# Attention with hashed buckets, then a mixture of experts: a group's first product with v issued one step earlier, and one more block transposed by DMA

## The chip, the cores and the metric

The kernel runs on one core of a Trainium2 chip. The metric is the device time of one execution in microseconds. The kernel before was timed three times: 747.42, 748.88 and 756.24 us, median 748.88 us. One further execution was profiled; its page and its trace are what this document reads.

Engines are named as in the profile: PE is the tensor engine (PEld its loading of weights), DVE is VectorE, ACT is ScalarE, POOL is GpSimd, and SP is the queue of SyncE, which issues most DMAs. L265 is line 265 of the kernel before.

## The reference

Attention with 4 batches, 8 heads, 768 positions and 64 channels per head. A query sees only the keys that fall into the same bucket, and the bucket is the sign pattern of six projections. The 512 channels of each of the 3072 tokens then go to one of 8 experts, the one with the largest gate logit.

```python
q_bits = (np.einsum('bhsd,dk->bhsk', q, proj) > 0)          # the same for k
mask = q_bucket[:, :, :, None] == k_bucket[:, :, None, :]
scores = np.where(mask, scale * np.matmul(q, k.transpose(0, 1, 3, 2)), -1e9)
attn = np.exp(scores - scores.max(-1)); attn = attn / (attn.sum(-1) + 1e-9)
x = np.matmul(attn, v)                       # [4, 8, 768, 64] -> [3072, 512]
expert_idx = np.argmax(x @ w_gate, axis=1)   # one expert of 8 for each token
out = gate_w * (np.maximum(x @ w1[e], 0) @ w2[e])            # e: the token's expert
```

## The kernel before

**Groups, blocks, steps.** Attention runs over 16 pairs of heads (`pr`, four pairs for each batch), and each pair over two halves of the queries (`g`). A pair and a half, written (pr, g), is a group; there are 32. A group has six blocks, (jj, hh): three tiles of 128 queries times the pair's two heads. A block is 128 queries by all 768 keys. The main loop (L752) takes one block a step, 192 steps in all; `n`, from 0 to 5, is the step inside its group.

**What a step issues.** Step i issues, in this order:

- turns that are due: DVE transposes a block that came back from a DMA (L256, into `pt`);
- what `later` holds for this step (DMAs of a moved block, the scaling of the sign bits on ACT);
- loads of v (step 0 of a second half) and of q and k for the pair after the next;
- the scores of block i + 2, called S here: four matmuls on PE (L225, L226) into one of two banks `s`, then the row maximum and two small operations on DVE (L228 to L230);
- the exponential of block i + 1 on ACT (L240), with its row sums;
- what `late` holds: ACT copies the finished product `o` to `ot` (L290) and adds 1e-9 to the row sums (L291);
- six PE transposes of block i, called T here (L265), three into each of two banks `t`, each three followed by a copy on ACT into `pt` (L268);
- at some steps a product with v (L283, `av`): 24 matmuls that add one query tile of the group before into the bank `o`;
- pieces of the routing (`timed`), then `out_and_route` when it is due, then what PREPARE lists for the next pair.

PE, DVE, ACT and SP take their instructions in exactly this order (a manual schedule); on POOL the work on q, k and the scattered rows is chained in the same order (`in_turn`).

**Blocks moved by DMA.** MOVES lists groups in which one or two blocks aren't transposed by PE. Their exponential is written as `pd`, four DMAs on SP write it to DRAM (L250, when the exponential's step begins), one DMA reads it back in another order two steps later (L253), and DVE finishes the transpose three steps after that (L256). In groups 2 to 7 the block of step 1 is moved, in groups 8 to 28 those of steps 1 and 3. `blocks` gives each group the order of its blocks and the order of its three products: (0, 1, 2) without moves, (1, 0, 2) with one move, (1, 2, 0) with two.

**Products.** The three products of a group stand in steps 1, 3 and 5 of the next group. In step 5, after the third, `av_evac` arranges the evacuation: for all groups but the last three it goes to `late`, so that ACT does it in step 0; for (14, 1) and (15, 0) DVE does it at once (L293, L301, L302). The list `divide` keeps the reciprocal of the row sums, and `out_and_route`, four steps after the evacuation was arranged, does whatever that list holds. There is one bank `o`.

**Routing.** After the last pair of a batch, `out_and_route` starts the gate logits of the half (L334, PE and a copy on ACT), and pieces follow at 1, 2, 3, 4, 5 and 7 steps: the output rows (L315, L316), gathering, the best expert (L358, L359), its one-hot (L363 to L367), ranks among the tokens (L373 to L384), and three scattered DMAs on POOL (L392). These fall into the first two pairs of the next batch. For the second half of the last batch the logits of three of the four pairs are made early (`early_logits`, L493 to L508), once (14, 1) is evacuated.

**Preparing the next pair.** PREPARE gives, for each step of a pair, which operands of the next pair are made: `q_operands` and `k_operands` on POOL, the projections and sign bits `pair_codes` (PE L148 into a bank `t`, DVE L150 into `cr`; ACT scales `cr` two steps later, L151), and `code_rows`, four DMAs on SP for each head (L176). For most pairs the codes are made in step 1 of the first half and the two heads' rows go out in step 4 and in step 0 of the second half.

**The rest.** Behind attention come the experts, two matrix products each in three passes, with weights loaded on SP and split on ACT and DVE (the first weights are split on DVE and POOL beside pairs 14 and 15: L679, L682).

Of the kernel before, what the change touches and what calls it, by code (L numbers as in the profile page):

```python
# [8 lines left out]
F32 = mybir.dt.float32  # L9
# [9 lines left out]
P = 128  # L19
B, H, S, D = 4, 8, 768, 64  # L20
NB = S // P
NPAIR = H // 2
# [35 lines left out]
def lsh_attention_moe_kernel(ctx, tc, qkd, q2d, k2d, v, pjbd, wg, w1, w2, ident_in, tri_in, cols_in, eoff_in, ids_in, out):  # L58
# [216 lines left out]
    late = []  # L275
    divide = []

# [8 lines left out]
    def av_evac(pr, g, sums, o, defer):  # L286
# [11 lines left out]
        if defer:  # L298
            divide.append(lambda: V.reciprocal(out=inv, in_=sums.rearrange("p (j h) -> p j h", h=2)))
        else:  # L300
            V.tensor_scalar(out=sums, in0=sums, scalar1=1e-9, scalar2=None, op0=ALU.add)  # L301
            V.reciprocal(out=inv, in_=sums.rearrange("p (j h) -> p j h", h=2))  # L302
# [210 lines left out]
    MOVES = {}  # L513
    for n in range(2, 2 * NPR - 3):
        MOVES[divmod(n, 2)] = (1, 3) if n >= 2 * NPAIR else (1,)
# [27 lines left out]
    for hh in range(2):  # L543
# [6 lines left out]
        {(0, 0): [(q_operands, (0,))], (0, 1): [(pair_codes, ()), (q_operands, (1,))], (0, 2): [(k_operands, (0,))], (0, 3): [(code_rows, (0,)), (k_operands, (1,))],  # L550
         (0, 4): [(code_rows, (1,))]})
    grp = {}
# [173 lines left out]
    def out_and_route(pr, g):  # L726
        while divide:
            divide.pop(0)()
        if pr % NPAIR < NPAIR - 1:
# [22 lines left out]
    for i, (pr, g, jj, hh) in enumerate(steps):  # L752
# [47 lines left out]
        for x in now:  # L800
            timed.remove(x)
            if x[1].__name__ == "gather_heads":
                x[1]()
        if prev is not None:
            if n == 0:
                o = ps_o.tile([P, 512], F32, name="o")
            order_p = blocks(prev[0], prev[1])[1]
            for jp in (order_p[:2], order_p[2:])[n] if last and n < 2 else order_p[n // 2:n // 2 + 1] if not last and n % 2 == 1 else ():
                av(prev[0], prev[1], jp, o)
            if n == (1 if last else 5):  # L810
                av_evac(prev[0], prev[1], prev[2], o, (prev[0], prev[1]) != (NPR - 2, 1) and not last)
                if not last:
                    due.append((i + 4, lambda a=prev[0], c=prev[1]: out_and_route(a, c)))
                if (prev[0], prev[1]) == (NPR - 2, 1):
                    light += early_logits(B - 1, 1)
        if n == 5:
            prev = (pr, g, sums)

        for x in now:
# [31 lines left out]
        if due and due[0][0] == i:  # L851
            due.pop(0)[1]()
        for f, x in PREPARE[2 if pr == NPR - 2 else min(pr, 1)].get((g, n), ()) if pr + 1 < NPR else ():
            f(pr + 1, *x)
# [376 lines left out]
```

## Time and profile before

| what | value |
|---|---|
| median of three runs | 748.88 us |
| profiled execution | 746.31 us |
| its span, first to last instruction | 744.5 us |
| mean granted clock of PE over the span | 0.993 |
| PE busy | 717.5 us, 96% |
| DVE, ACT, POOL busy | 527.4, 457.9, 384.5 us |
| idle time of PE | 27 us: 744.5 less 717.5 |

Attention takes the first 460 us, with the routing between the batches; the experts take the rest. A row of a timeline gives the start in us, the busy time in us, the engine, the line, the operation, the tile written and the tiles read, the shape, the number of merged instructions, and in brackets the idle time of that engine just before and what ended it. Starts of PE's instructions are records, their ends are modelled, so distances are best taken from start to start. Some PE records also overlap: a matmul starts while the one before it drains.

### The profile page before, as it was taken

The page shows a single profiled execution, that of the slowest core. Times are in us where ns is not written, and L with a number is a line of the kernel's source. Part 1 is how long each engine was busy: PE and PEld are TensorE (multiplying, and loading weights), DVE is VectorE, ACT ScalarE, POOL GpSimd, SP SyncE. Part 2 cuts the span into 40 slices and gives each one's busy share as a digit, 9 for nine tenths or more (in the row PEclk, how much of TensorE's full clock was granted, in tenths as well). Part 3 has the DMA queues.
Part 4 walks back from the last instruction along what each step waited for, and adds up shares of the span by engine and source line. Part 5 has one row for each costly group of instructions (what it writes and reads, how often), then busy time and mean ns, then how long its engine had stood idle before and what let it go on. Part 6 is the DMA issues. An engine that isn't in the chain of part 4 may idle for free.

```text
span 744.5 us, 16345 instructions
## 1 busy us (share of the span) xinstructions
PE 717.5 (96%) x5919; PEld 632.3 (85%) x5919; DVE 527.4 (71%) x1158; ACT 457.9 (62%) x941; POOL 384.5 (52%) x366
## 2 busy tenths in 40 slices
PE   6999999999999999999989998999999999999996
PEld 3788888877888778888777887999999999999994
DVE  6667776887887888887899776674747465566741
ACT  5888887777888678888677865343434334344430
POOL 2877337098436187634485242007474738364381
PEclk8999999999999999999999999999999999999999
DMA  5166666666666567666664531746556565657531
GB/s 185 50 192 165 195 182 189 187 194 189 178 183 190 170 203 196 166 181 188 176 180 131 160 90 59 209 105 177 146 175 152 189 165 161 188 154 226 165 91 43
DMA packets 85259, 121.45 MB, mean 163 GB/s; under 512 B 10758, under 2 KB 57382, under 8 KB 85168
## 3 DMA queue, kind: packets, MB, share of 16 engines
q1 hardware_dynamic: 80176, 107.61, 51.3%
q0 software_dynamic: 4992, 12.69, 4.9%
q8 instruction: 49, 0.80, 0.5%
q14 instruction: 42, 0.34, 0.1%
HBM read 79.04 MB, written 39.24 MB: 159 GB/s over the span
## 4 chain that ended last, share of the span: by engine, by line
PE 45%; issue 22%; POOL 13%; DVE 11%; DMA 5%; SPq 2%; ACT 1%; POOLq 0%; DVEq 0%
PE o L283 14%; POOL y L1007 10%; PE t L265 9%; PE s L225 9%; PE s L226 7%; DVE m L228 4%; DMA y<-yo,tags 2%; POOL yo L1005 1%; PE misc L315 1%; PE t L148 1%; DMA qk<-qkd 1%; DMA xr<-xs 1%; DVE m L230 1%; SPq L176 1%; ACT p L240 1%
## 5 line engine op out<-in xcount | busy, mean ns | idle before, releaser
L228 DVE TENSOR_REDUCE m<-s 128x1 f32<-128x768 f32 x192 | 182.6, 951 | 48.4 <-PE s L226 41.4
L240 ACT ACTIVATE p<-s,m 128x768 f32<-128x768 f32 x144 | 143.3, 995 | 42.0 <-DVE m L230 27.8
L225 PE MATMUL s<-k,q 128*128 128x512 f32 (+1 forms) x384 | 149.2, 389 | 7.8 <-ACT p L240 5.2
L283 PE MATMUL o<-pt,vt 128*64 128x128 f32 x2304 | 146.7, 277 | 0.2
L268 ACT COPY pt<-t 128x384 f32<-128x384 f32 x288 | 123.9, 482 | 34.3 <-PE t L265 31.2
L283 PEld LDWEIGHTS o<-pt,vt 128*64 128x64 f32 x2304 | 123.8, 137 | 14.8 <-issue 7.4
L226 PE MATMUL s<-k,q 76*128 76x512 f32 (+1 forms) x384 | 123.9, 343 | 0.2 <-DVE q L218 0.2
L265 PE MATMUL t<-ident,p 128*128 128x128 f32 x864 | 120.0, 274 | 3.2 <-DVE cr L150 3.1
L1007 POOL DMA_INDIRECT y<-yo,tags x89 | 103.3, 1161 | 25.2 <-issue 22.9
L225 PEld LDWEIGHTS s<-k,q 128*128 128x128 f32 x384 | 73.2, 191 | 44.4 <-issue 15.0
L265 PEld LDWEIGHTS t<-ident,p 128*128 128x128 f32 x864 | 99.0, 141 | 6.7 <-DVE cr L150 4.0
L965 ACT ACTIVATE hh<-hps 128x352 fp32r<-128x352 f32 (+3 forms) x56 | 28.0, 500 | 99.3 <-PE hps L979 88.6
L682 DVE TENSOR_TENSOR wlo<-wraw,whi 128x1024 fp32r<-128x1024 f32 x60 | 73.0, 1219 | 17.0 <-ACT whi L677 16.0
L226 PEld LDWEIGHTS s<-k,q 76*128 76x128 f32 x384 | 73.7, 192 | 9.3 <-ACT k L201 0.5
L998 PE MATMUL hps<-hh,wlo 128*128 128x436 f32 (+6 forms) x224 | 76.2, 340 | 0.0
L998 PE MATMUL hps<-hh,whi 128*128 128x448 f32 (+10 forms) x224 | 76.2, 340 | 0.0
L998 PE MATMUL hps<-hl,whi 128*128 128x436 f32 (+6 forms) x224 | 76.2, 340 | 0.0
L979 PE MATMUL hps<-xh,whi 128*128 128x352 f32 (+3 forms) x224 | 75.0, 335 | 0.0
L979 PE MATMUL hps<-xh,wlo 128*128 128x428 f32 (+6 forms) x224 | 74.8, 334 | 0.0
L979 PE MATMUL hps<-xl,whi 128*128 128x428 f32 (+6 forms) x224 | 74.8, 334 | 0.0
L1005 POOL TENSOR_TENSOR yo<-yt,tags 128x512 f32<-128x512 f32 (+3 forms) x25 | 23.4, 959 | 88.1 <-DVE yt L1000 88.0
L966 DVE SCALAR_TENSOR_TENSOR hl<-hps,hh 128x352 fp32r<-128x352 f32 (+3 forms) x56 | 31.7, 566 | 48.6 <-ACT hh L965 45.0
(225 smaller groups left out, 1202.1 us busy)
## 6 DMA issues: line engine op xcount, KB each, us to landing
wraw<-w SPq DMA_DIRECT2D x64, 512.0 KB
moved<-pd SPq DMA_DIRECT2D x192, 96.0 KB
pq<-moved SPq DMA_DIRECT2D x48, 384.0 KB
qk<-qkd SPq DMA_DIRECT2D x30, 384.0 KB
xs<-zrow SPq DMA_DIRECT2D x8, 910.0 KB
vt<-v SPq DMA_DIRECT2D x16, 384.0 KB
xr<-xs SPq DMA_DIRECT2D x12, 178.8 KB
xr<-xs SPq DMA_DIRECT2D x8, 227.5 KB
```

Source lines behind the costliest of these rows:

```text
L225: PE.matmul(out=s[:, c0:c1], lhsT=q1[:, qs], rhs=k1[:, c0:c1], start=True, stop=False)
L226: PE.matmul(out=s[:, c0:c1], lhsT=q2[0:KM, qs], rhs=k2[0:KM, c0:c1], start=False, stop=True)
L228: V.reduce_max(out=m[:, 0:1], in_=s[:, 0:S], axis=AX.X)
L240: A.activation(to, of, AF.Exp, bias=m[:, 2:3], scale=m[:, 1:2], accum_out=sums[:, idx:idx + 1])
L265: PE.transpose(out=t[:, i * P:i * P + P], in_=p[:, kc * P:kc * P + P], identity=ident)
L268: A.copy(out=dst, in_=src)
L283: PE.matmul(out=o[hh * D:hh * D + D, jj * P:jj * P + P], lhsT=vt[:, kc, hh * D:hh * D + D], rhs=pt[:, hh, kc], start=kc == 0, stop=kc == N ...
L682: loeng.tensor_tensor(out=lo[:, i:i + step], in0=cell["t"], in1=bf(hi[:, i:i + step]), op=ALU.subtract)
L966: V.scalar_tensor_tensor(out=hl, in0=hps[:, 0:C], scalar=0.0, in1=bf(hh), op0=ALU.max, op1=ALU.subtract)
L979: PE.matmul(out=hps[:, 0:w], lhsT=wt[:, c, fs], rhs=xt[:, c, 0:w], start=n == 0, stop=n == 3 * NDC - 1)
L998: PE.matmul(out=yps[:, 0:w], lhsT=wt[:, f, ds], rhs=ht[:, 0:w], start=n == 0, stop=n == 3 * NFC - 1)
L1007: rows_apart("out", G.indirect_dma_start(out=out_seg, out_offset=bass.IndirectOffsetOnAxis(ap=tags[:, i, 0:1].bitcast(I32), axis=0), in_=y ...
```

## The change

The first of a group's three products is issued in step 5 of the group itself, behind the T of that step; `o` is allocated there. The other two stand in steps 1 and 3 of the next group. The evacuation is arranged in step 3, so that ACT does it in step 4. `out_and_route` comes six steps after that instead of four, which is the same step as before; since two groups' reciprocals can now be pending, `divide` is keyed by group. For the last group the two products left of the group before stand in its steps 0 and 1, where three stood.

Group (0, 1) joins MOVES, with the block of its step 1. Its blocks and its products then follow the order of the groups with one move. There are 49 moved blocks instead of 48.

For pairs 5, 9 and 13 PREPARE makes the codes of the next pair in step 3 of the first half instead of step 1, and the first head's code rows go out in step 5 instead of step 4.

```diff
-    divide = []
+    divide = {}
...
-            divide.append(lambda: V.reciprocal(out=inv, in_=sums.rearrange("p (j h) -> p j h", h=2)))
+            divide[(pr, g)] = lambda: V.reciprocal(out=inv, in_=sums.rearrange("p (j h) -> p j h", h=2))
...
-    for n in range(2, 2 * NPR - 3):
+    for n in range(1, 2 * NPR - 3):
         MOVES[divmod(n, 2)] = (1, 3) if n >= 2 * NPAIR else (1,)
...
-         (0, 4): [(code_rows, (1,))]})
+         (0, 4): [(code_rows, (1,))]},
+        {(0, 0): [(q_operands, (0,))], (0, 1): [(q_operands, (1,))], (0, 2): [(k_operands, (0,))], (0, 3): [(pair_codes, ()), (k_operands, (1,))],
+         (0, 5): [(code_rows, (0,))], (1, 0): [(code_rows, (1,))]})
...
-        while divide:
-            divide.pop(0)()
+        if (pr, g) in divide:
+            divide.pop((pr, g))()
...
-        if prev is not None:
-            if n == 0:
-                o = ps_o.tile([P, 512], F32, name="o")
-            order_p = blocks(prev[0], prev[1])[1]
-            for jp in (order_p[:2], order_p[2:])[n] if last and n < 2 else order_p[n // 2:n // 2 + 1] if not last and n % 2 == 1 else ():
-                av(prev[0], prev[1], jp, o)
-            if n == (1 if last else 5):
+        at = (0, 1) if last else (1, 3)
+        if prev is not None and n in at:
+            av(prev[0], prev[1], blocks(prev[0], prev[1])[1][1 + at.index(n)], o)
+            if n == at[1]:
                 av_evac(prev[0], prev[1], prev[2], o, (prev[0], prev[1]) != (NPR - 2, 1) and not last)
                 if not last:
-                    due.append((i + 4, lambda a=prev[0], c=prev[1]: out_and_route(a, c)))
+                    due.append((i + 6, lambda a=prev[0], c=prev[1]: out_and_route(a, c)))
...
         if n == 5:
             prev = (pr, g, sums)
+            if not last:
+                o = ps_o.tile([P, 512], F32, name="o")
+                av(pr, g, blocks(pr, g)[1][0], o)
...
-        for f, x in PREPARE[2 if pr == NPR - 2 else min(pr, 1)].get((g, n), ()) if pr + 1 < NPR else ():
+        for f, x in PREPARE[2 if pr == NPR - 2 else 3 if pr > NPAIR and pr % NPAIR == 1 else min(pr, 1)].get((g, n), ()) if pr + 1 < NPR else ():
```

## The prediction

> **What bounds the kernel now.** I read the page first, then busy time by stage, then the timelines of single steps. The page's engine line and its TensorE slices:
>
> ```profile
> PE 717.5 (96%) x5919; PEld 632.3 (85%) x5919; DVE 527.4 (71%) x1158; ACT 457.9 (62%) x941; POOL 384.5 (52%) x366
> ...
> PE   6999999999999999999989998999999999999996
> ```
>
> TensorE (PE) is busy 717.5 of 744.5 us. The change removes almost no work from it, so it can win only where PE stands idle, and there is little of that: the first slice, the last, and the 8s in the middle. Busy time of stretches that I cut at the score products shows where the 8s lie (columns: length, then PE, PEld, DVE, ACT, POOL busy with counts, clock, DMA share, GB/s): an ordinary pair (pair 6), then pairs 4 and 5, which follow a batch's end and carry its routing.
>
> ```profile
> 178.54:203.77 25.23, 25.23 (x256) 21.51 (x254) 20.54 (x45) 20.78 (x46) 14.07 (x14) 1.00 0.61 173
> ...
> 120.81:178.54 57.73, 54.42 (x544) 44.59 (x542) 47.00 (x126) 42.51 (x95) 33.00 (x31) 1.00 0.66 194
> ```
>
> Pair 6 has no PE idle time at all. Two pairs with routing take 57.73 instead of 2 x 25.23 = 50.46 us and hold 3.31 us of idle time. In the ordinary stage an operation that is only moved costs or wins nothing unless it makes PE wait.
>
> **The first groups.** The change puts the first product with v of group (0,0) into its own step 5, behind that step's transposes, and lets the block of step 1 of group (0,1) be moved by DMA. PE's timeline there (S = L225 with L226, T = L265, product = L283):
>
> ```profile
> 26.34 0.82 PE L265 MATMUL t<-ident,p 128*128 128x128 f32 x6
> 27.89 0.50 PE L225 MATMUL s<-k,q 128*128 128x512 f32 x1 [0.73 <-ACT p L240]
> ...
> 28.71 0.82 PE L265 MATMUL t<-ident,p 128*128 128x128 f32 x6
> 29.62 0.50 PE L225 MATMUL s<-k,q 128*128 128x512 f32 x1
> ...
> 30.43 0.82 PE L265 MATMUL t<-ident,p 128*128 128x128 f32 x6
> 31.18 1.53 PE L283 MATMUL o<-pt,vt 128*64 128x128 f32 x24
> 32.64 0.50 PE L225 MATMUL s<-k,q 128*128 128x512 f32 x1
> ```
>
> ```profile
> 30.47 0.99 ACT L240 ACTIVATE p<-s,m 128x768 f32<-128x768 f32 x1
> ```
>
> ScalarE paces this stretch, and PE waits. Start to start, S to T is 0.82 (27.89 to 28.71), T to product 0.75 (30.43 to 31.18), product to S 1.46 (31.18 to 32.64). T to S, where nothing waits, is 0.55 (in pair 10, below, T to T is 1.37, less 0.82). After the change: T at 26.34, product at 27.09, S at 28.55, T at 29.37, S at 29.92, no T, product 0.82 later at 30.74, next S at 32.2. Today that S starts at 32.64 with one product done; then it would start 0.44 earlier with two done. It also needs the exponential of the block whose S is at 27.89, which starts 2.58 behind that S (30.47): with S at 28.55 it runs from 31.13 to 32.12, and its sum is read a little later, so I put that S at 32.4. The gain is 1.46 + 0.24 = 1.7 us. It stays, because PE's slices from there to the first 8s are full and every group still holds three products; it is cashed where the last group has one product less in front of it. Bounds: 1.46 + 0.44 = 1.9 if that exponential comes sooner; a loss of 0.7 if the whole delay of S (28.55 for 27.89) falls on the chain and the early product is worth nothing. I take 1.7, since every step of it is in these rows.
>
> The move itself adds one turn on VectorE, four writes and one read on SP's queue.
>
> ```profile
> L256 DVE STREAM_TRANSPOSE pt<-pq x48: 967/969/979, 54.3 to 413.7; 128x768 f32<-128x768 f32 x48
> ...
>   DMA pq<-moved: 2.2, 3
> ```
>
> ```profile
> 32.39 0.71 SPq L176 DMA_DIRECT2D k<-cr  x1
> ...
> 42.46 1.78 SPq L250 DMA_DIRECT2D moved<-pd  x4
> ```
>
> The turn is 0.97 us in group (1,0), where it replaces ScalarE's two copies; of 48 turns 3 waited for their read, 2.2 us together. The four writes (1.78 in the row above, those of step 1 of (1,0)) will stand on SP ahead of the second head's code rows, whose last now goes out by 33.10, of the loads of pair 2 and a prefill; all of these become some 2 us later. The second head's first S is in step 0 of (1,0), a step ahead of the writes at 42.46, so near 40: 5 us of cover remain. If it were gone, PE would lose what is missing, once: 0 to 2 us, taken as 0.
>
> **The ordinary groups.** Products stay in steps 1, 3 and 5, so PE's load by step is the same. Two things get tighter. First, ot and the sums are evacuated in step 4 instead of step 0, ahead of that step's copies, and step 5 turns again at once. PE and then ScalarE in pair 10:
>
> ```profile
> 295.65 0.82 PE L265 MATMUL t<-ident,p 128*128 128x128 f32 x6
> ...
> 297.02 0.82 PE L265 MATMUL t<-ident,p 128*128 128x128 f32 x6
> ```
>
> ```profile
> 295.02 0.99 ACT L240 ACTIVATE p<-s,m 128x768 f32<-128x768 f32 x1 [0.24 <-DVE inv L299]
> ...
> 296.18 0.86 ACT L268 COPY pt<-t 128x384 f32<-128x384 f32 x2
> ...
> 299.05 1.01 ACT L240 ACTIVATE pd<-s,m 128x768 f32<-128x768 f32 x1
> ...
> 300.03 0.49 ACT L290 COPY ot<-o 128x384 f32<-128x384 f32 x1
> 300.39 0.24 ACT L291 ACTIVATE sums<-sums 128x6 f32<-128x6 f32 x1
> 300.58 0.86 ACT L268 COPY pt<-t 128x384 f32<-128x384 f32 x2
> ```
>
> Behind an exponential, ot starts after 0.98 (299.05 to 300.03) and the copies 0.55 later. In step 4 that would put the copies at 295.02 + 1.53 = 296.55 instead of 296.18: 0.37 late. The pair of copies ends at 297.04 now; its first half frees a bank near 296.7, and T of step 5 starts at 297.02 with its second half some 0.3 later: 0.3 of slack for 0.37 of delay. All but the last three of the 32 groups are evacuated this way. Between 0 and the 0.07 that these numbers leave I take 0.02 us, 0.5 over 29 groups, since a copy that waits for its T loses less than one that ScalarE paces. Bounds: 0 if the slack holds, 29 x 0.37 = 10.7 us if it is gone.
>
> Second, the product of the moved block stands in step 3 instead of 5, one step behind its turn. In group (6,1):
>
> ```profile
> 195.38 0.97 DVE L256 STREAM_TRANSPOSE pt<-pq 128x768 f32<-128x768 f32 x1
> ...
> 197.65 1.53 PE L283 MATMUL o<-pt,vt 128*64 128x128 f32 x24
> ```
>
> The turn ends at 196.35, and the product that stands there now begins at 197.65: 1.3 us of cover. Behind that product on PE's queue stands the S of step 4, and the exponential behind that waits with it. In (5,0), below, the cover is 0.6. Only a read landing over 0.6 late would show, and then VectorE itself waits with it, as today. Price 0, up to 2.2 us (today's waits once more).
>
> **The pairs with routing.** In pairs 5, 9 and 13 the sign bits (pair_codes) go from step 1 to step 3, the first code rows from step 4 to 5. Group (5,0), VectorE and then PE:
>
> ```profile
> 155.88 0.62 DVE L150 TENSOR_SCALAR cr<-t,cols 128x384 fp32r<-128x384 f32 x1
> 156.41 0.97 DVE L256 STREAM_TRANSPOSE pt<-pq 128x768 f32<-128x768 f32 x1
> ...
> 161.12 0.56 DVE L316 TENSOR_TENSOR xr<-misc,inv 128x384 f32<-128x384 f32 x1
> 161.59 0.95 DVE L228 TENSOR_REDUCE m<-s 128x1 f32<-128x768 f32 x1
> ```
>
> ```profile
> 153.35 0.85 PE L148 MATMUL t<-qk,pj 128*32 128x384 f32 x8
> ...
> 156.55 0.55 PE L265 MATMUL t<-ident,p 128*128 128x128 f32 x3 [0.94 <-DVE cr L150]
> ...
> 157.97 1.53 PE L283 MATMUL o<-pt,vt 128*64 128x128 f32 x24
> 159.75 0.52 PE L315 MATMUL misc<-ident,ot 128*128 128x128 f32 x3 [0.24 <-DVE slot L384]
> 160.02 0.48 PE L225 MATMUL s<-k,q 128*128 128x512 f32 x1
> ...
> 162.17 0.50 PE L225 MATMUL s<-k,q 128*128 128x512 f32 x1 [0.53 <-ACT p L240]
> ```
>
> T waits 0.94 us for a bank that cr still holds. Without cr in step 1, VectorE is 0.53 ahead (155.88 to 156.41) until step 3. But the projection (0.85 of PE, 153.35) is moved too, behind L315, which waits for VectorE. L315 then starts at 159.75 - 0.53 = 159.22, the projection 0.27 later, S at 160.34 instead of 160.02 and its T at 161.16; xr starts at 160.59, cr behind it near 161.1 and is done at 161.7. T's second bank waits for that instead of 161.45, and the S of 162.17 starts at about 162.0. Late next is cr again, two steps on. I take 0 for each of the three pairs; bounds 0.5 worse (cr's 0.53 now stands ahead of step 4's maximum) to 0.94 + 0.53 = 1.47 better (both waits gone). On SP the code rows wait for ScalarE's scaling in step 5, with the load of v and the second head's rows behind them; their first use is five steps on.
>
> **The end.** The product with v of (14,1) ends two steps earlier, so the early logits leave step 5 of (15,0), where PE waits for ot.
>
> ```profile
> 437.24 0.83 PE L493 MATMUL misc<-ot,wg_sb 128*32 128x384 f32 x2 [0.43 <-DVE ot L293]
> ...
> 439.57 2.84 PE L283 MATMUL o<-pt,vt 128*64 128x128 f32 x48
> ```
>
> ```profile
> 436.64 0.55 DVE L293 COPY ot<-o 128x384 f32<-128x384 f32 x1
> 437.10 0.79 DVE L301 TENSOR_SCALAR sums<-sums 128x6 f32<-128x6 f32 x1
> ```
>
> Of the two products at 439.57 one is already done, which is the gain counted above; the 0.43 us of waiting go as well. Against it, ot, L301 and the reciprocal come into step 3 of (15,0), beside the casts of w1. L301 took 0.79 for 6 columns. [...] From the rows alone: gain 0.43, less 0 to 0.8. I take 0.4.
>
> **Sum.** 1.7 + 0.4 - 0.5 = 1.6 us less. The profiled execution took 746.31 (span 744.5 and 1.8 around it), which gives 744.7. The median of the runs, 748.88, is 2.57 above the profiled one, so 747.3.
>
> **Rivals.** (1) Slower: the evacuation in step 4 makes T of step 5 wait. It decides from the point where the copies come over 0.3 us later than now. For it: 0.37 against 0.3. Against: a copy that waits for T loses less, and 0.3 covers most of the 0.37. Half its bound, 29 x 0.18 = 5.3, gives 747.3 + 4.8 = 752.1, the whole 757.5. (2) Faster: in pairs 5, 9 and 13 the wait really goes, 3 x 1.47 = 4.4: 742.9. For it: VectorE is the late engine there. Against: PE's moved projection. (3) The early start is worth nothing: the S that slips by 0.66 carries through ScalarE, and only the 0.43 and the 0.5 remain: 749.0. For it: ScalarE paces those steps. Against: one turning and its copies are gone there.
>
> **How the numbers follow.** Forecast 0.5, rival (1) 0.18, (2) 0.17, (3) 0.15. The range 742.0 to 752.0 holds the forecast, (2), (3) and the half of (1) in which less than half the slack is missing: about 0.9, less some 0.1 for the runs' own spread (747.42 to 756.24). About 2%, 15 us, is what a measurement of this kernel can tell from no change; even rival (1) in full stays inside it. Faster by over 2%: 0.02; within: 0.95; slower: 0.03, for a stall of every group that no row shows.
>
> **What would show it.** Right: no idle of 0.73 near 27.9; L256 x49 and L265 x858; one product, not two, ahead of the second S of the last group; no wait of L493 for ot. Rival (1): L265 waiting for L268 in step 5. Rival (2): pairs 4 and 5 clearly under 57.73. Rival (3): two products ahead of the S that now starts at 32.64, and that S over a microsecond later. The prediction is wrong if ordinary pairs leave 25.23, or if L283 waits for L256.

## The result and the profile after

The changed kernel is slower. Its median is 760.01 us (751.69 to 761.63, seven executions) against 750.41 us (747.42 to 758.11, seven) for the kernel before in the same series: a ratio of 1.0119, 95% interval 1.0079 to 1.0158. The prediction was 747.3 us, range 742.0 to 752.0. These numbers can't be understood without the clock: six of the seven executions of the changed kernel show a mean clock of TensorE (PE) of 0.980 to 0.983 and 759.51 to 761.63 us, while the profiled one has 0.992 and 751.69 us, so its trace shows only part of the loss, 5.38 us over the 746.31 profiled before.

The page of the changed kernel, engines and PE's slices:

```profile
PE 720.6 (96%) x5913; PEld 632.9 (84%) x5913; DVE 526.8 (70%) x1159; ACT 455.0 (61%) x939; POOL 387.9 (52%) x366
...
PE   6999999999999899999899998999999999999996
...
PEclk9999999999999999999989999999999999999999
```

PE is busy 3.1 us longer, with six transposes (one T) fewer, and its clock has a dent in the middle that the page of before does not have (that one has an 8 in its first slice). Busy time by stretches cut at S (length, then PE, PEld, DVE, ACT, POOL busy, clock, DMA share, GB/s) shows where. The kernel before, pairs 4 and 5, 8 and 9, 12 and 13, then pairs 6 and 7, then group (15,1):

```profile
116.44:174.17 57.73, 54.43 (x545) 44.59 (x544) 46.91 (x125) 42.11 (x94) 32.91 (x31) 1.00 0.69 203
224.67:281.77 57.10, 54.39 (x545) 44.60 (x544) 47.51 (x126) 42.38 (x94) 33.42 (x32) 1.00 0.64 187
332.27:390.32 58.05, 54.46 (x546) 44.58 (x544) 48.77 (x126) 42.45 (x95) 33.73 (x33) 1.00 0.63 183
174.17:224.67 50.50, 50.50 (x508) 43.02 (x509) 42.39 (x92) 41.67 (x91) 27.82 (x25) 1.00 0.62 178
431.61:451.15 19.54, 19.11 (x202) 15.12 (x201) 13.80 (x34) 10.94 (x24) 6.73 (x6) 1.00 0.24 74
```

The changed kernel, the same five:

```profile
115.12:172.72 57.60, 54.87 (x545) 44.67 (x544) 46.76 (x125) 41.48 (x94) 32.82 (x31) 1.00 0.65 197
223.69:281.83 58.14, 54.72 (x546) 44.63 (x544) 48.66 (x126) 41.94 (x95) 33.70 (x33) 1.00 0.61 182
332.68:393.80 61.12, 57.33 (x545) 46.50 (x544) 47.55 (x126) 42.05 (x95) 33.66 (x33) 0.94 0.59 174
172.72:223.69 50.97, 50.97 (x509) 42.97 (x509) 42.40 (x92) 41.44 (x91) 27.76 (x25) 1.00 0.62 179
435.45:454.02 18.57, 17.27 (x178) 13.78 (x177) 13.17 (x34) 10.94 (x24) 6.77 (x6) 1.00 0.25 79
```

The changed kernel comes into pair 4 1.32 us ahead, wins 0.97 in the last group, and loses 4.0 in the three routed stretches (-0.13, +1.04, +3.07) and 0.47 in four ordinary groups. The last S ends 2.87 us later than before (454.02 for 451.15), and 2.5 us more are lost behind it: PE waits 0.80 us there for the late rows of the first expert (0.08 before), the rest was not traced. The 3.07 holds a halved clock, which follows a window in which PE waited 1.56 us for a bank. Halved for 6.82 us while PE works all through, it costs up to half of that, 3.4 us, by estimate:

```profile
369.60:373.02 3.42, 1.86 (x17) 1.45 (x14) 3.14 (x14) 2.00 (x4) 3.28 (x4) 1.00 0.72 225
373.02:379.84 6.82, 6.80 (x45) 4.44 (x44) 4.67 (x14) 3.71 (x11) 6.43 (x7) 0.50 0.78 228
```

### The profile page after: what moved, and what is told of

Its sections match the earlier page's. It is cut to its first block, busy times and chain, and to the rows that moved or that the text cites. A ratio compares the mean times of both kernels' runs of the same rounds, so it can differ in the third digit from the quotient of the medians.

```text
span 749.9 us, 16376 instructions
## 1 busy us (share of the span) xinstructions
PE 720.6 (96%) x5913; PEld 632.9 (84%) x5913; DVE 526.8 (70%) x1159; ACT 455.0 (61%) x939; POOL 387.9 (52%) x366
## 5 line engine op out<-in xcount | busy, mean ns | idle before, releaser
L228 DVE TENSOR_REDUCE m<-s 128x1 f32<-128x768 f32 x192 | 182.6, 951 | 52.0 <-PE s L226 39.7
L283 PE MATMUL o<-pt,vt 128*64 128x128 f32 x2304 | 148.3, 278 | 0.0
L1009 POOL DMA_INDIRECT y<-yo,tags x89 | 105.7, 1188 | 25.2 <-issue 22.6
L265 PEld LDWEIGHTS t<-ident,p 128*128 128x128 f32 x858 | 97.1, 141 | 4.9 <-issue 1.9
```

The lines of the kernel that those rows point to most:

```text
L228: V.reduce_max(out=m[:, 0:1], in_=s[:, 0:S], axis=AX.X)
L265: PE.transpose(out=t[:, i * P:i * P + P], in_=p[:, kc * P:kc * P + P], identity=ident)
L283: PE.matmul(out=o[hh * D:hh * D + D, jj * P:jj * P + P], lhsT=vt[:, kc, hh * D:hh * D + D], rhs=pt[:, hh, kc], start=kc == 0, stop=kc == N ...
L1009: rows_apart("out", G.indirect_dma_start(out=out_seg, out_offset=bass.IndirectOffsetOnAxis(ap=tags[:, i, 0:1].bitcast(I32), axis=0), in_=y ...
```

## The experiments

They ran in five series, each on one chip with the kernel before beside it; its medians were 739.07, 752.77, 737.85, 737.72 and 737.53 us. "Low" below counts the executions with a mean clock under 0.99.

### First series: the parts alone

The first theory came from the dent above: idle time of PE in the routed pairs brings the clock down. Four kernels hold parts of the change: all but the codes' place, the codes' place alone, the shifted products alone, the moved block alone.

```diff
# e1_codes_back, against the kernel after
-        for f, x in PREPARE[2 if pr == NPR - 2 else 3 if pr > NPAIR and pr % NPAIR == 1 else min(pr, 1)].get((g, n), ()) if pr + 1 < NPR else ():
+        for f, x in PREPARE[2 if pr == NPR - 2 else min(pr, 1)].get((g, n), ()) if pr + 1 < NPR else ():
# e2_codes_only: the kernel before with that line of the kernel after, and its fourth table
# e3_products_only: e1 with     for n in range(2, 2 * NPR - 3)
# e4_move_only: the kernel before with     for n in range(1, 2 * NPR - 3)
```

> The changed kernel with the sign bits of pairs 5, 9 and 13 back in step 1 and their first code rows back in step 4; products, evacuation and the move of (0,1) as changed. Theory A (clock): the moved sign bits leave the tensor engine idle for 1.56 us in one stretch of pair 13's group (13,0), and its clock is then halved for 6.83 us there, and in most runs in pairs 5 and 9 as well; with the bits back no halved clock between 30 and 740 us, granted clock 0.99, and 746 to 751 us. Theory B (ScalarE): the evacuation in step 4 and the shifted products cost the time; then this stays at 757 to 761. Theory C (the moved block of (0,1)): also 757 to 761.

> The kernel before with only the sign bits of pairs 5, 9 and 13 moved to step 3 (first code rows to step 5). Theory A: granted clock 0.98 in most runs, halved stretches of 6.83 us near pairs 5, 9 and 13, 756 to 761 us. Theories B and C: as before, 747 to 751, clock 0.99.

> The kernel before with only the first product in step 5, the others in steps 1 and 3, and the evacuation in step 4. Theory A: 747 to 752, clock 0.99; against before about 1 us more in the groups with two moved blocks and 1 us less at the start. Theory B: 757 to 761. Theory C: as before.

> The kernel before with only the block of step 1 of group (0,1) moved by DMA. Theories A and B: 0.5 to 1 us less than before in the first two pairs, 746 to 751 us, clock 0.99. Theory C: 757 or more.

Measured: 738.31 us (ratio 0.9997, 0.9913 to 1.0081), 738.85 (0.9995, 0.9921 to 1.0068), 743.12 (1.0011, 0.9914 to 1.0108), 737.19 (0.9983, 0.9898 to 1.0069). Low: 1 of 4, 0 of 4, 2 of 4, 1 of 4, and 2 of 7 for the kernel before. None is told apart from it, and the kernel before has low executions too: the low clock is not new with the change.

### Second series: the changed kernel again, and idle time filled

```diff
# f1_changed_again: the kernel after.  f2_codes_back_again: e1.
# f3_changed_filled and f4_before_filled: the kernel after and before, with
+        if pr > NPAIR and pr % NPAIR == 1 and n in (1,):
+            fill(pr, o, 4)      # 4 x PE.matmul(out=o[:, 384:512], lhsT=q1[:, 0:P], rhs=k1[:, 0:P], start=True, stop=True)
```

> The changed kernel unchanged, beside the kernel before and the three kernels below on one chip. Three theories. Theory A (clock): the routed pairs 5, 9 and 13 of the changed kernel leave TensorE idle in one piece (0.92, 1.49 and 1.56 us ahead of an S, L225, in its trace), its clock is then halved for 6.83 us at a time, and most executions show a mean clock near 0.98 and some 9 us more than the others. Theory A expects that on any chip: most runs of this kernel at 0.98, median 7 to 10 us above the kernel before. Theory D (late releases): in the first pair of traces VectorE's L228 begins 1.0 to 1.8 us after TensorE's S in 5 places, each beside a scattered write (L392); the traces of the four kernels of the first series, taken on another chip, hold no such place. The changed order meets these late releases worse (group (13,0) took 18.32 for 16.10 us). Theory D expects 3 to 6 us more than before if this chip shows late releases in the trace, and nothing (within 2 us) if it shows none. Theory C (luck of the executions): the share of runs with the lower clock is the same as with the kernel before, about 3 in 10, and the medians agree within 3 us.

> The changed kernel with the codes of pairs 6, 10 and 14 computed in step 1 as before and their rows written in steps 4 and (1,0): products and move stay changed. If the place of the codes is the cause (theories A and D both allow it: in the first series this kernel's trace has no idle time of 0.9 us or more of TensorE in pairs 5, 9 and 13, against 0.92 to 1.56 in the changed kernel's), it is within 2 us of the kernel before, and faster than the changed kernel beside it by what that one loses. If the products' shift is the cause, it is as slow as the changed kernel. Theory C: no difference between the two.

> The changed kernel with four extra products of TensorE (128x128, about 0.28 us each) into columns of the o tile that nothing reads, behind the product of step 1 of the six groups of pairs 5, 9 and 13: they fill the idle time ahead of the next S. They cost at most 6 x 1.1 = 6.6 us, less what they fill (0.92 + 1.49 + 1.56 in the g = 0 groups). Theory A expects the mean clock back at 0.99 or above in most runs, and so a median below the changed kernel's by 2 to 7 us. Theory D expects the same clocks as the changed kernel and 1 to 4 us more time. Theory C: the clocks fall as often as before, time 1 to 4 us longer.

> The kernel before with the same extra products in the same six groups: the control. Its idle time there lies elsewhere (ahead of T of a later step), so hardly any is filled: up to 6.6 us longer in runs of the same clock. Theory A expects no more runs at the lower clock than with the kernel before, perhaps fewer. Theories C and D expect the same share.

Measured: 761.63, 761.72, 760.44 and 750.03 us beside 752.77, with ratios of 1.0036 (0.9953 to 1.0119), 0.9951 (0.9858 to 1.0045), 1.0077 (1.0019 to 1.0136) and 0.9961 (0.9908 to 1.0014); low 5 of 6, 4 of 6, 5 of 6, 0 of 6, and 6 of 11 before. The low clock is there again on another chip, it stays when the codes go back, and filling the routed pairs does not cure it. As the cause of the low executions the first theory falls. But on this chip the kernel before is low about half the time as well, so f1 alone does not tell the two apart; and that f4 has no low execution was not followed up.

In a smaller way the first theory holds. Behind a wait of PE in the routed pairs, or in the pair after them, the clock is halved for 3.4 to 6.8 us in three of the eight traces with the codes moved (at 373.0 us above, at 266.7 in f1, at 182.6 in g1 of the third series) and in none of the twelve others. In f1 PE had waited 1.52 us for a bank:

```profile
266.70:270.11 3.41, 3.40 (x22) 2.99 (x24) 3.20 (x10) 1.92 (x5) 3.21 (x4) 0.50 0.75 206
```

So the end of the last S, 453.79 us in f1 and 451.03 in f2, gives no price of the codes: f1 has 10.24 us of halved clock ahead of it, f2 3.41, and half of the difference, up to 3.4 us by estimate, can come from that alone.

The profile of f1 is one of a low execution. Its windows show where the clock goes:

```profile
461.24:464.65 3.41, 1.87 (x16) 1.56 (x16) 1.55 (x17) 0.49 (x4) 1.93 (x2) 1.00 0.58 227
464.65:468.07 3.42, 3.42 (x16) 3.42 (x15) 1.59 (x13) 2.25 (x6) 1.92 (x2) 0.50 0.22 85
468.07:481.72 13.65, 12.12 (x90) 11.26 (x90) 8.39 (x34) 2.21 (x6) 1.34 (x3) 1.00 0.57 148
481.72:502.20 20.48, 20.48 (x93) 20.28 (x94) 8.21 (x12) 5.86 (x11) 0.40 (x2) 0.50 0.44 119
```

One stretch of 20.48 us at half speed, at the beginning of the first expert and far from the routed pairs; PE works all through it, so it costs about 10 us, half of it, by estimate. f3's trace has the same stretch, 478.92 to 499.40. Ahead of it PE stands idle, for the late rows of the first expert. That expert's first 288 tokens come from the first three batches; their products with its weights are called early. The rest, the late ones, are complete only with the last batch: SP reads them (`xrl`) when its rows have been scattered, DVE turns them, ACT makes `xh`, and the first late product follows. PE and DVE of f1:

```profile
479.54 0.34 PE L715 MATMUL s<-xh,whi 128*128 128x160 f32 x1 [1.45 <-ACT xh L626]
```

```profile
478.79 0.57 DVE L625 STREAM_TRANSPOSE xt<-xrl 128x160 f32<-128x160 f32 x2 [3.35 <-DMA xrl<-xs]
```

and DVE of the kernel before, where PE waited 0.08 us at that point:

```profile
473.19 0.57 DVE L623 STREAM_TRANSPOSE xt<-xrl 128x160 f32<-128x160 f32 x2 [1.60 <-DMA xrl<-xs]
```

The queues of the DMA engines while the 640 packets of these rows are on their way (count, MB, share of the engines' time), kernel before from 469.99 to 472.71 us:

```profile
q1 hardware_dynamic: 704, 0.33, 54.4%
```

and f1 from 473.82 to 477.72 us:

```profile
q1 hardware_dynamic: 809, 0.55, 55.7%
q8 instruction: 1, 0.02, 1.5%
```

A piece of 16 KB of code (0.79 MB in 48 pieces on the page of the changed kernel) falls into the reading, and weights queued behind the rows get in between (809 packets for 704). The reading takes 4.84 us from the first issue to the last packet, for 3.67 in the kernel before. That is half of the delay. The other half stands ahead of it: SP waits for the last scattered write, and issues the reading 19.09 us after the last S, for 17.89. In f3 the code is not in the reading at all: the piece came from 17.75 to 19.34 us, the reading was issued at 20.89 and took 3.36 us, and PE waited 1.14 us before its clock fell. SP of f3, whose last S ends at 450.77:

```profile
471.66 1.97 SPq L645 DMA_DIRECT2D xrl<-xs  x4
```

That the code is PE's is an estimate by its number: 48 such pieces a run for 2 x 5913 instructions, 246 each, and DVE, the next engine, has 1159 instructions. Its place shifts with the number of PE's instructions ahead of it: f3's 24 extra products and their 24 loads of weights brought the piece to 17.75 us after the last S, for 19.89, 20.42 and 22.06 in the kernel after, f2 and f1.

This gave the second theory, E1. Its first step: the new order brings the piece of code into the reading, the rows come late, and PE waits for them. Its second step: behind that wait the clock falls for the long stretch. f3 shows that rows which are late for another reason end in the same way.

### Third series: the code moved, the gap filled or made

```diff
# g1_changed_code_early (kernel after), g2_codes_back_code_early (e1): ahead of the first work of PE
+    small = ps_m.tile([P, 512], F32, name="misc")
+    for _ in range(64):
+        PE.matmul(out=small[0:32, 0:1], lhsT=ones[0:32, 0:32], rhs=ones[0:32, 0:1], start=True, stop=True)
# g3_changed_rows_filled (kernel after): ahead of the late products
+    for _ in range(24):
+        PE.matmul(out=first_h[7][:, 448:512], lhsT=w1_first[0][0][:, 0, 0:P], rhs=x_first[0][1][0][:, 0, 0:64], start=True, stop=True)
# g4_before_made_idle (kernel before)
-    for n in ("01010101012", 2, "201", 3, "01", 22, "20101222222", 96, "22"):
+    for n in ("01010101012", 2, "201", 3, "01", 22, "20101222222", 63, "22"):
...
                 for f, done in first_products(1):
+                    if f == 1:
+                        some_products(6)
```

> The changed kernel with 64 tiny products of TensorE (32x32 by 32x1, two instructions each) at the very start, where TensorE waits 4.22 us for its first load: 128 instructions ahead of all others. New theory, from the traces of the second series. Step 1: TensorE's code comes in pieces of 16 KB (queue 8); one of them lands 17.8 us after the end of the last S in the kernel before, and at 19.9, 22.1 and 20.4 us in three traces of kernels with the shifted products, amid the 640 packets of 520 B that bring the late rows of the first expert (18.5 to 23.9 us); these rows then come 0.4 to 1.5 us later, and TensorE, which has run out of early products, stands idle for 0.64 to 1.45 us ahead of the first late product (L715; 0.08 in the kernel before). Step 2: where TensorE had been idle at L429 and is idle here again, its clock is halved for 20.48 us some 4 to 6 windows later (481.72 to 502.20 us in the changed kernel's second trace), which costs 8 to 10 us. [...] Theory E1 (code collides with the rows): idle ahead of the first late product under 0.4 us, mean clock at 0.99 or above in most executions, median 749 to 754 us. Theory E2 (the rows are late for another reason that comes with the shifted products): idle 0.6 to 1.5 us, clock 0.98 in most, median 758 to 763 us.

> The changed kernel with the codes of pairs 6, 10 and 14 back in step 1 and with the 64 tiny products at the start. In the second series the codes' place moved the end of the last S by 2.8 us (453.79 us changed, 451.03 with the codes back, 451.15 before). Theory E1: idle ahead of the first late product under 0.4 us, median 747 to 750 us, 2 to 3 us below the kernel above and 1 to 3 below the kernel before. Theory E2: 758 to 762 us.

> The changed kernel with 24 extra products of TensorE (128x64, about 0.07 us each, 1.7 us together) into columns that nothing reads, behind the last early product and ahead of the first late one, where TensorE stands idle in it. The rows come no sooner. If that idle time is what gets the clock halved (step 2 of the theory), no halved stretch of 20 us follows: mean clock 0.99 or above, median 751 to 755 us (0.2 to 1 us of extra work). If the clock falls for another reason, 0.98 and 759 to 764 us.

> The kernel before with the last 6 early products (0.29 us each) put behind the first 13 late ones: no work is added, but TensorE reaches the first late product 1.7 us sooner than its rows, and stands idle for that long in a kernel without the changed order. If such idle time gets the clock halved, most executions show a mean clock near 0.98 and the median is 758 to 763 us. If not, the idle time itself is all: 1 to 2 us above the kernel before.

Measured beside 737.85 us: 741.45 (1.0048, 1.0025 to 1.0070), 737.18 (0.9986, 0.9968 to 1.0004), 744.09 (1.0039, 1.0008 to 1.0071), 740.15 (1.0034, 1.0004 to 1.0064). Low: 0 of 11, 0 of 11, 5 of 12, 1 of 11, and 5 of 34 before. With the 64 products at the start the piece of code begins 9.90 to 10.12 us after the last S, ahead of the reading (table below), the rows arrive earlier, and PE doesn't wait for them; DVE of g1:

```profile
468.67 0.57 DVE L625 STREAM_TRANSPOSE xt<-xrl 128x160 f32<-128x160 f32 x2 [1.19 <-DMA xrl<-xs]
```

g3 was a miss of the second step: PE's gap was filled, and the clock fell all the same, out of a window without idle time:

```profile
471.00:474.46 3.46, 3.46 (x34) 3.46 (x33) 2.23 (x8) 1.46 (x5) 0.38 (x2) 1.00 1.17 244
474.46:498.35 23.89, 23.89 (x105) 23.47 (x104) 10.60 (x16) 8.85 (x14) 0.40 (x2) 0.50 0.34 101
```

The 24 narrow products (64 columns) took 0.11 us each from start to start, as long as the late products with 148, so the columns did not set that time; PEld was busy for all 3.46 us of the window above. g4's 0.87 us of idle time go with 1 low execution of 11, no more than in the kernel before.

Between g1 and g2 only the codes differ, and no execution of either is low: their place costs 741.45 - 737.18 = 4.3 us on this chip. It is not lost in the routed pairs but in the pair behind them. Pairs 4 and 5, then 6 and 7, in g1 and in g2:

```profile
115.06:170.53 55.47, 54.43 (x546) 44.63 (x544) 46.91 (x125) 41.71 (x95) 31.38 (x31) 1.00 0.67 198
170.53:224.91 54.38, 52.23 (x512) 44.35 (x510) 42.09 (x90) 41.61 (x91) 29.23 (x26) 0.97 0.61 175
...
114.18:169.99 55.81, 54.42 (x546) 44.52 (x544) 46.97 (x125) 41.98 (x95) 31.72 (x31) 1.00 0.68 200
169.99:220.79 50.80, 50.80 (x511) 42.98 (x510) 42.10 (x90) 41.40 (x91) 28.88 (x26) 1.00 0.63 181
```

On SP's queue in g1:

```profile
164.36 0.73 SPq L176 DMA_DIRECT2D k<-cr  x1
165.14 0.59 SPq L140 DMA_DIRECT2D vt<-v  x1
165.78 0.76 SPq L176 DMA_DIRECT2D q<-cr  x1
166.59 0.71 SPq L176 DMA_DIRECT2D k<-cr  x1
167.35 0.71 SPq L176 DMA_DIRECT2D q<-cr  x1
168.11 0.71 SPq L176 DMA_DIRECT2D k<-cr  x1
168.93 2.11 SPq L250 DMA_DIRECT2D moved<-pd  x4
```

The four writes of group (5,1)'s moved block stand behind all eight code rows in both kernels. In g1 the first of these rows goes out at 161.73 us (157.23 in g2), and the writes at 168.93 us (165.72 in g2, which is 0.5 us ahead in all there). DVE then waits for the block, its maxima stand behind that turn, and PE waits for ScalarE:

```profile
178.17 0.98 DVE L256 STREAM_TRANSPOSE pt<-pq 128x768 f32<-128x768 f32 x1 [3.81 <-DMA pq<-moved]
```

```profile
181.66 0.50 PE L225 MATMUL s<-k,q 128*128 128x512 f32 x1 [2.15 <-ACT p L240]
```

In g2 the same turn waits 1.00 us, and PE does not wait there:

```profile
174.82 0.98 DVE L256 STREAM_TRANSPOSE pt<-pq 128x768 f32<-128x768 f32 x1 [1.00 <-DMA pq<-moved]
```

Behind its 2.15 us of waiting PE's clock is halved in g1, for 3.41 us, so up to 1.7 us of the loss in this trace is clock, by estimate:

```profile
182.59:186.00 3.41, 3.41 (x21) 2.99 (x21) 2.96 (x5) 2.74 (x7) 0.94 (x2) 0.50 0.77 205
```

DVE's waits for moved blocks add up to 10.0 us in g1 and 1.6 in g2. In the other traces of the series 1, 3 and 4 they are 6.3 to 12.8 us with the whole change (g3, h1, h3) and 1.5 and 2.2 with shifted products and the codes back (e1, e3). The sum is no mark of the codes alone: with products and codes in place it is 5.0 to 11.5 us too (g4, h2, h4, i1, i2; 1.9 in e4). So the shifted products seem to take most of these waits away, and the moved codes to bring them back; e4 does not fit. In the second series the sums do not differ (1.2 in f1, 1.1 in f2), and no price of the codes is shown there.

### Fourth series: the reverse, and wide products in the gap

```diff
# h1_changed_third: the kernel after.  h2_before_code_late: the kernel before, as g1 with range(104)
# h3_changed_products_twice (kernel after), ahead of the late products
+    wh, wl = w1_first[0][:2]
+    xh, xl = x_first[0][1][0], x_first[0][2][0]
+    n = 0
+    for c in range(NDC):
+        for wt, xt in ((wh, xh), (wh, xl), (wl, xh)):
+            PE.matmul(out=first_h[7][:, 0:E0], lhsT=wt[:, c, 7 * P:8 * P], rhs=xt[:, c, 0:E0], start=n == 0, stop=n == 3 * NDC - 1)
+            n += 1
# h4_before_held_11: g4 with 58 and some_products(11)
```

> The changed kernel unchanged once more, as the base of the three kernels beside it: in the third series (another chip than the second) none of 11 executions with the early code had a mean clock under 0.99, and the changed kernel itself was not run there. Theory E1 (a piece of TensorE's code of 16 KB comes amid the late rows): idle of 0.4 to 1.5 us ahead of the first late product, clock under 0.99 in 4 to 9 of 10 executions, slower than the changed kernel with the early code (741.45 us there) in the median or in the upper half. If the early code changed nothing, it shows the same times as that one: 737 to 742 us, with no clock under 0.99.

> [...] Theory E1: rows 0.4 us or more later, idle ahead of the first late product, clock under 0.99 in 4 to 9 of 10 executions, median up to 10 us above the kernel before. If the code's place doesn't matter: as the kernel before, within 1.5 us, clock under 0.99 in 1 to 3 of 10.

> The changed kernel in which the last group of 12 early products (128x288, 0.133 us from start to start, 1.6 us) is done a second time ahead of the first late product, with the same result. In the third series 24 products of 64 columns in this place did not keep the clock up (5 of 12 executions under 0.99; 474.46 to 498.35 us halved in the trace, with no idle time): they took 0.113 us each from start to start, as the late products of 148 columns do, so most of that time was loading of weights. If the clock follows the columns that TensorE streams, and not only its idle time, wide products in the gap keep it up: clock at 0.99 or above in 9 of 10, and up to 1.2 us of extra work, 738 to 744 us on a chip with the times of the third series. If rows that come late make the clock fall in another way, 4 to 9 of 10 under 0.99 as in the changed kernel beside it.

> The kernel before with the last 11 early products (0.133 us each from start to start, 1.5 us together) behind the first 13 late ones; 6 of them made 0.87 us of idle time and 1 in 11 executions under 0.99. Now idle time should be 1.3 to 1.7 us, as in the changed kernel's worst trace (1.45). If idle time in this place is what brings the clock down, 4 to 9 of 10 executions are under 0.99 and the median is 4 to 10 us above the kernel before. If not: 1 to 2 us above, and 1 to 2 of 10.

Measured beside 737.72 us: 741.06 (1.0050, 1.0008 to 1.0092), 737.87 (0.9994, 0.9973 to 1.0016), 740.75 (1.0030, 1.0008 to 1.0052), 739.78 (1.0046, 1.0000 to 1.0092). Low: 4 of 11, 0 of 11, 0 of 11, 2 of 11, and 6 of 33 before.

- h1 is the base: here too the changed kernel loses its clock, in 4 of 11.
- h2 was to bring the piece of code amid the late rows in the kernel before, and missed that aim in a telling way. The piece began at 19.13 us after the last S and the rows were complete at 19.16, earlier than in the kernel before: nothing had met them. It is a third kernel with the early rows, and a third without a low execution.
- h3 has the rows as late as h1 has them, and wide products in the gap: 0 of 11 low for 4 of 11. Chance alone makes such a split about once in eleven, so this is a sign and not a proof.
- h4 has 1.36 us of idle time in the kernel before and no more low executions than that one has. Idle time alone is not enough; there 11 wide products follow 13 late ones, so narrow work lasts for 2.4 us (465.43 to 467.87 us in its trace) instead of some 11 after the gap.

When the rows were complete, and when the piece of code began, from the packets of the traces (us after the end of the last S; the chips of series 1, 3, 4 and 5, where the reading is always issued at 15.95 to 15.98):

```
                                code begins    rows complete  PE idle ahead of late products
products in place (e2 e4 g4 h4) 15.84..16.79   19.82..19.93   0.04, 0.10; 0.87, 1.36 (made)
products shifted (e1 e3 h1)     18.03..18.30   20.28..20.40   0.46..0.60
the same, gap filled (g3 h3)    19.07, 18.32   20.82, 20.31   0
code out of the way (g1 g2 i1 i2 and h2)
                9.90..10.12 and 19.13          19.14..19.34   0
```

The first step of E1 rests on this table: a piece of code in the way makes the rows 0.5 to 1.7 us later. With the products in place it meets the four issues and not the packets: SP's next issue follows 0.60 us after the piece has ended, in each of these four traces (in e2 at 17.89 us, for 17.10 where no code is in the way); what holds SP is not shown. One rival is left for the second step: all five kernels with the code out of the way begin with the tiny products, and no run parts these from the place of the code.

### Fifth series: the parts without the code in the way

```diff
# i1_move_code_early: e4 with g1's 64 products.  i2_before_code_early: the kernel before with them.
```

> The kernel before with one part of the change, the moved block of group (0,1), and with the 64 tiny products at the start. By the traces so far the moved block wins 1.3 to 2 us (the last S ends at 443.32 us with it and at 444.4 to 444.9 us in two traces without it, on chips with the same times), and with the piece of code ahead of the late rows no execution under a mean clock of 0.99 is expected. 2.5 to 4 us below the kernel before in the mean of all executions, 1 to 3 us in the median of the undisturbed ones, and 1 to 2.5 us below the kernel beside it. Shorter than both kernels of the study.

> The kernel before with the 64 tiny products alone, the control. The piece of code of 16 KB comes some 7 us earlier than in the kernel before (16 to 18 us after the last S there), so ahead of the late rows: these end at 19.1 to 19.3 us after the last S (19.8 to 19.9 in the kernels with the products in place), no idle time ahead of the first late product, no execution under 0.99 (17 of 67 would be expected by the share of the kernel before in the last two series, 11 of 67). Undisturbed executions within 1 us of the kernel before.

Measured beside 737.53 us: 737.16 (0.9994, 0.9975 to 1.0014) and 737.59 (0.9999, 0.9980 to 1.0017); low 0 of 12, 0 of 12, and 0 of 23 before. A miss: on this chip the kernel before has no low execution either, so i2 says nothing on the clock, and the moved block wins 0.43 us, not 1 to 2.5. No version is shown to beat the kernel before.

## Why the prediction was wrong

Of the 12.7 us between the forecast and the median, 7.0 lie in the profiled execution (751.69 for 744.7) and 5.75 in the distance from it to the median (8.32 for the 2.57 added).

**The start and the end.** The start was right in kind. Traces with the same clock there have group (1,0) 0.4 us ahead of the kernel before's, counted from the first S (29.48 and 29.44 for 29.88 and 29.92 us); the forecast was 0.24. Of the 1.32 us of lead above, most is a stretch of half clock that was 3.41 instead of 6.83 us long, which is luck. At the end the saved product was to bring 1.46 us, and the wait of L493 another 0.4. That second term had the wrong sign: the wait grew from 0.43 to 1.30, and the last group is shorter by 0.97 only.

```profile
438.36 0.85 PE L493 MATMUL misc<-ot,wg_sb 128*32 128x384 f32 x6 [1.30 <-DVE xr L316]
```

Together that is 1.4 us for the 2.1 forecast. VectorE has the output rows ahead of what the early logits need, and these logits now stand a step sooner.

**The ordinary groups** were undersized: 0.47 us over the four groups of pairs 6 and 7, 0.12 each, for the 0.02 taken. No group stalls as rival (1) had it. If all 29 groups lose as much, that is some 3.4 us, an estimate, for the 0.5 taken, and more than the start and the end win.

**The routed pairs** are the first step that failed. The prediction took 0 for each, with 0.5 worse as the bound; the profiled execution loses 4.0 us in the three stretches. Up to 3.4 of it is the halved clock behind PE's wait in pair 13, which the prediction had no term for: a wait cost its own length there and no more. On another chip the loss comes in the pair behind (g1: 54.38 us for 50.80 in pairs 6 and 7, while pairs 4 and 5 win 0.34). SP had been put aside with "their first use is five steps on". That holds for the code rows, but what is queued behind them had to be asked too: the moved block of the pair's second group. There the codes' place costs 4.3 us in the median (g1, g2), halved clock included. With no low execution at all (g1) the changed kernel is slower by 0.48%. With the codes back as well (g2) the rest of the change is not told from the kernel before (ratio 0.9986, 0.9968 to 1.0004), for the 1.6 us forecast.

**From the profiled execution to the median** is the second and dearer step. The prediction added 2.57 us, the distance in the kernel before, as if it were the same for both. The changed kernel's distance is that of a profiled execution without the low clock from a median with it: 6 of its 7 executions are low, and 5 of 6 and 4 of 11 in f1 and h1, for 6 of 11 and 6 of 33 of the kernel before beside these. On neither chip alone is the difference beyond chance; the three comparisons point the same way (two of the kernel before's seven in the result lie over 756 us).

What makes an execution low is shown in part. In the three traces of low executions (f1, f3, g3) the long halved stretch lies behind the first late product of the first expert. With the rows of that expert early, no execution of the changed order is low (0 of 22 in g1 and g2), while 5 of 12 are with late rows and narrow products in the gap on the same chip (g3); against the kernel before there (5 of 34) the 22 alone would not be clear. With late rows and wide products in the gap none is low either (0 of 11 in h3, for 4 of 11 in h1). That it takes narrow products behind a gap is only argued: in f1, f3 and g3 the clock fell 3.6 to 4.2 us after the last wide product began, and h4's mixture did not do it. That it is the code which makes the rows late holds for the chips of the table. On the chip of the second series the late scattered write does as much (f1) or all (f3), and of the low executions of the result none was traced, so their cause stays open.

The stretches of half clock quoted here are 3.41 to 3.42, 6.82, 20.48 and 23.89 us long. Ahead of them PE was busy, by records whose ends are modelled, for 1.86 of 3.42 us (the changed kernel, from 369.60), 1.87 and 2.10 of 3.41 us (f1, from 461.24 and 478.31) and all of 3.46 us (g3, from 471.00). These traces don't show how much idle time a fall of the clock takes.

## What to carry over

A distance between a profile and a median is a property of one kernel, not a constant: ask which executions make it. Where a queue is moved past, list everything behind the moved instruction until the queue runs empty, and who waits for the last of it. And a reordering of PE also moves its code: with the products in place the piece in the table above begins 15.84 to 16.79 us after the last S, with the products shifted 18.03 to 18.30. A hand-over that fits to 0.1 us (in the kernel before the cast of the late rows begins at 473.57 us, and the first late product stands 0.08 us behind its predecessor) can be lost by that: PE waits 0.46 to 0.60 us in e1, e3 and h1, and not at all in g1 and g2.

## What the runs showed of the hardware

- **Code takes time of the DMA engines, and a read beside it ends later.** The page of the changed kernel counts the pieces that are put down to PE as one line among the queues:

```profile
q8 instruction: 48, 0.79, 0.5%
```

  Half a percent of the engines' time, yet one piece amid a small read that others wait for delays it: from 19.14 to 19.34 us to 20.28 to 20.40 in the table above, and in the second series from 3.23 and 3.36 us between first issue and last packet (f4, f3) to 4.38 and 4.84 (f2, f1). Where the piece meets the four issues instead (e2, e4, g4, h4), SP's next issue follows 0.60 us after it has ended. PE itself shows no wait for its code there: four pieces fall into pairs 6 and 7 of the kernel before, and PE is busy for all of their 50.50 us.
- **The clock can fall while PE's records show no gap**: in g3 behind a window that is busy for 3.46 of 3.46 us, most of it narrow products and the loading of their weights (PEld 3.46 us too). That the loading is the reason is not shown.
- **Chips differ in how soon DVE starts behind PE.** On the chips of the first pair of traces and of the second series DVE's maximum (L228) begins 1.0 to 1.8 us after its S, with DVE idle, in three or four places, each beside a scattered write (L392); in the other traces there is no such place. In the same traces SP issues the late rows 17.57 to 20.89 us after the last S, for 15.95 to 15.98 in the others. What causes it stays open. It may be part of why the kernel before takes some 750 us there and 738 us here.
